# Loading the first rows in three pieces, splitting the first feed-forward slab by columns, and moving the rest columns behind the folded weights

## The chip, the cores and the metric

The kernel runs on one core of one Trainium2 chip. The metric is the device time of one execution in microseconds (us). It is some 1.3 us longer than the span that a profile shows, from the first instruction to the last. The first 512-column matmuls start 0.427 us apart and not 0.216 as later. "The clock turns" is said here for the change from the one step to the other.

## The reference

Two branches work on the same `x` (2048 tokens, 512 wide), and a gate mixes them. Cut to what matters:

```python
qkv = x @ wqkv                                   # 512 -> 3*512, 32 heads of 16
pq, pk = q @ w_phi, k @ w_phi                    # per head, 16x16
phi = concat(softmax(p), softmax(-p))            # for q and for k
kv, z = phi_k^T v, sum(phi_k)                    # over all tokens
a = (phi_q kv / (phi_q z + 1e-6)) @ wo           # linear attention
b = relu(x @ w1) @ w2                            # 512 -> 1376 -> 512
g = sigmoid(sum(x * gate_w))
out = g * a + (1 - g) * b
```

## The kernel before

The kernel is tuned. TensorE is kept busy from the first microsecond to the last; the other engines copy, exponentiate and normalise behind it. Two stages are touched by the change.

**The start.** The first 512 rows of `x` ("x0") are loaded plainly, in two halves, and transposed by TensorE (a matmul against the identity), because the transposing loads would come too late (the first one of `x` lands at 18.9 us). VectorE and ScalarE copy the transposed pieces from PSUM to `XT`. Then the first eight 128-column units of `x @ w1` are computed "slab by slab": slab `t` multiplies the `t`-th quarter of the inner dimension for all eight units, so that a slab needs only one row block of `w1`. All eight PSUM banks are in use, so a bank that held a transposed piece is free for its unit only after that piece has been copied.

```python
warm(5)                       # matmuls on constants, until data arrive
...
ea = xtr("a0", 0, (0, 1), 6, (("dve", 0, 1, "xa0"), ("dve", 1, 2, "xa1")))
c1 = ("a1", 0, (2, 3), 7, (("act", 0, 2, "xa2"),))
xtr(*c1, part=(0, 1))
eb = xtr("b0", 1, (0,), 2, (("act", 0, 1, "xb0"),))
ec = xtr(*c1, part=(2, 3))
ed = xtr("b1", 1, (1, 2), 1, (("act", 0, 2, "xb1"),))
...                           # the copies are emitted here
slab(0, range(4))             # 512 columns, units 0 to 3
for fn in xtr("b2", 1, (3,), 2, (("dve", 0, 1, "xb3"),)):   # bank 2: unit 6 waits for this copy
    fn()
slab(0, range(4, 8))
...
for t in range(1, NDT):
    slab(t)
```

**The folded weights.** `wq` and `wk` are multiplied by `w_phi` once ("pre", eight results, the even ones copied by VectorE and the odd ones by ScalarE). The first q/k tile (`atile(0)`) needs all eight copies. Value tiles (`vtile`) and the rest columns of `w1` with the gate column (`rest`) are put between as work that doesn't depend on them.

```python
hunit(0, 8)
hunit(0, 9, "dve")
vtile(0, "dve")
vtile(1, "act", nextbank())
for i in range(4):
    pre(i)
rest(0)
for i in range(4, 8):
    pre(i)
vtile(2, "dve")
...
for m in range(NT):
    atile(m)                  # first q/k tile for m == 0
    ...
```

The softmax here doesn't subtract the row's maximum and nothing guards it: scores larger than these inputs give would overflow.

## Time and profile before

| | before |
|---|---|
| median of the first three executions | 147.16 us |
| the execution that was profiled | 148.19 us (span 146.80) |
| TensorE busy | 143.2 us, 98% of the span |
| share of the chain of waits on TensorE | 95% |

The first lines of the profile's page for the kernel before (span, TensorE's busy time with its share and its count of instructions, and the chain of work that ended last, followed back from the last instruction, by engine; PE is TensorE, PEld its weight loads, DVE VectorE, ACT ScalarE, POOL GpSimd, SP the engine that issues the loads):

```profile
span 146.8 us, 2520 instructions
...
PE 143.2 (98%) x961; PEld 73.2 (50%) x978; DVE 92.3 (63%) x157; ACT 72.7 (49%) x125; POOL 52.0 (35%) x62
...
PE 95%; DMA 2%; DVE 1%; issue 1%; SPq 0%
```

TensorE bounds the kernel, so only its idle time and its slow time can be won. The timeline of the kernel before shows where those lie. Its columns are the start, the length of the merged stretch, engine, line, operation, output and input with their form, the count, and in brackets the idle time before with what ended it.

```profile
2.90 0.85 PE L239 MATMUL PS<-IDN,OT 128*128 128x128 bf16 x6
...
3.97 1.04 PE L239 MATMUL PS<-IDN,OT 128*128 128x128 bf16 x8 [0.22 <-DMA OT<-in_A_x_dram]
...
4.93 1.60 PE L528 MATMUL PS<-XT,W 128*128 128x512 bf16 x4
...
6.67 0.42 DVE L255 CAST XT<-PS 128x256 bf16<-128x256 f32 x1 [2.35 <-PE PS L239]
...
16.64 1.22 DVE L321 CAST WQK<-PS 128x480 bf16<-128x480 f32 x2 [0.38 <-PE PS L316]
...
17.07 0.86 PE L294 MATMUL PS<-W,XT 128*128 128x97 bf16 x16
17.72 0.88 PEld L316 LDWEIGHTS PS<-Wbd,PHQ 128*128 128x128 bf16 x16
17.77 1.00 PE L316 MATMUL PS<-Wbd,PHQ 128*128 128x120 bf16 x16
...
18.18 1.22 DVE L321 CAST WQK<-PS 128x480 bf16<-128x480 f32 x2 [0.31 <-PE PS L316]
...
18.82 0.81 PE L411 MATMUL PS<-WV,XT 128*128 128x512 bf16 x3
...
19.59 1.78 PE L336 MATMUL PS<-WQK,XT 128*128 128x480 bf16 x8
19.67 0.69 DVE L419 CAST VS<-PS 128x512 bf16<-128x512 f32 x1 [0.27 <-PE PS L411]
```

Three readings. The transposes (L239) wait for the second half of x0 at 3.97. The first four 512-column matmuls (L528, from 4.93) span 1.60 us, which is twice as slow as later. Two VectorE copies of folded weights run from 18.18 to 19.40, and the first q/k matmul (L336) starts right behind, at 19.59; VectorE copies value tile 2 (L419) only after them.

Starts of single instructions in the trace give the gaps exactly. Matmuls overlap in the trace (a 512-column one is shown 0.379 us long at the full clock), so gaps are read from start to start: two 512-column matmuls in a row start 0.216 us apart at the full clock and 0.427 us apart before it turns. TensorE has four gaps in the whole execution: 0.43 and 0.13 us before the first slab, 0.25 us at 6.9, 0.12 us at 19.5. (A single step of 0.43 us here and there later is taken for a missing record and not a gap: the page counts 978 weight loads but 961 matmuls.)

### The profile page before, as it was taken

To read this page: it belongs to the slowest core of one execution; us is meant where nothing else is said; L and a number is where in the kernel's file an instruction comes from. 1 tells how busy PE (TensorE), PEld (TensorE's weight loads), DVE (VectorE), ACT (ScalarE), POOL (GpSimd) and SP (SyncE) were. 2 spreads that over 40 slices of the span, in tenths; PEclk is the share of its full clock that TensorE was granted. 3 is DMA by queue.
4 is the path that set the end of the run, shared out by engine and by line. 5 is a ranking of instruction groups with operands and counts; after the bars stand their busy time and mean duration, and the time that the engine had idled before them with its cause. 6 is when DMAs were issued, how large, how long until landed. Compare 5 with 4: busy or idle time off the path is not lost.

```text
span 146.8 us, 2520 instructions
## 1 busy us (share of the span) xinstructions
PE 143.2 (98%) x961; PEld 73.2 (50%) x978; DVE 92.3 (63%) x157; ACT 72.7 (49%) x125; POOL 52.0 (35%) x62
## 2 busy tenths in 40 slices
PE   8999999999999999999999999999999999999994
PEld 3444744444545545555645555554444444444443
DVE  3327746777688778678698976675444555555342
ACT  3307547887778778877878863022222111111150
POOL 2040001788768678787868820300000000000000
DMA  6999991033449965335843531454343322322213
GB/s 197 295 258 214 180 263 23 0 71 71 76 86 304 178 198 92 71 71 107 43 107 71 107 71 21 90 107 110 74 94 82 75 71 67 80 71 74 71 44 106
DMA packets 45221, 16.12 MB, mean 110 GB/s; under 512 B 39352, under 2 KB 44568, under 8 KB 45208
## 3 DMA queue, kind: packets, MB, share of 16 engines
q1 hardware_dynamic: 45056, 15.92, 49.6%
q8 instruction: 8, 0.13, 0.4%
q10 hardware_dynamic: 152, 0.03, 0.1%
q14 instruction: 5, 0.04, 0.1%
HBM read 4.41 MB, written 2.10 MB: 44 GB/s over the span
## 4 chain that ended last, share of the span: by engine, by line
PE 95%; DMA 2%; DVE 1%; issue 1%; SPq 0%
PE PS L490 25%; PE PS L282 19%; PE PS L336 18%; PE PS L499 9%; PE PS L411 9%; PE PS L528 5%; PE PS L465 3%; PE PS L433 3%; DMA OT<-in_A_x_dram 2%; PE PS L294 2%; PE PS L316 1%; PE PS L239 1%; DVE WQK L513 1%; DVE XT L255 0%; SPq L162 0%
## 5 line engine op out<-in xcount | busy, mean ns | idle before, releaser
L490 PE MATMUL PS<-W,HT 128*128 128x512 bf16 (+4 forms) x181 | 40.0, 366 | 0.3
L379 POOL TENSOR_TENSOR EB<-EB,SC 128x1024 bf16<-128x1024 bf16 x15 | 28.9, 1927 | 25.0 <-DVE SC L377 25.0
L355 ACT ACTIVATE EB<-PS 128x480 bf16<-128x480 f32 (+1 forms) x44 | 30.1, 757 | 15.1 <-PE PS L336 15.1
L504 ACT ACTIVATE TFA<-PS,GT 128x512 bf16<-128x512 f32 x16 | 11.0, 687 | 42.7 <-PE PS L499 36.6
L282 PE MATMUL PS<-XT,W 128*128 128x512 bf16 x124 | 30.0, 379 | 0.2
L336 PE MATMUL PS<-WQK,XT 128*128 128x480 bf16 x128 | 28.5, 366 | 0.0
L375 DVE TENSOR_REDUCE ZB<-EB 128x64 f32<-128x1024 bf16 x15 | 18.3, 1220 | 14.0 <-ACT EB L355 14.0
L513 DVE SCALAR_TENSOR_TENSOR WQK<-PS,OMG,TFA 128x512 bf16<-128x512 f32 (+2 forms) x17 | 12.2, 719 | 23.6 <-ACT TFA L504 22.4
L490 PEld LDWEIGHTS PS<-W,HT 128*128 128x128 bf16 (+1 forms) x187 | 17.0, 98 | 17.4
L268 ACT ACTIVATE HT<-PS 128x512 bf16<-128x512 f32 x35 | 20.3, 616 | 7.6 <-PE PS L528 5.7
L336 PEld LDWEIGHTS PS<-WQK,XT 128*128 128x128 bf16 x128 | 12.5, 98 | 14.0 <-DVE WQK L321 0.4
L390 DVE TENSOR_REDUCE ZB<-EB 128x64 f32<-128x1024 bf16 x16 | 18.6, 1164 | 0.0
L282 PEld LDWEIGHTS PS<-XT,W 128*128 128x128 bf16 x128 | 12.0, 98 | 13.2
L399 POOL TENSOR_TENSOR EB<-EB,SC 128x512 bf16<-128x512 bf16 x16 | 16.9, 1056 | 1.3
L499 PE MATMUL PS<-WO,OT 128*128 128x512 bf16 x63 | 16.0, 378 | 0.1
L411 PE MATMUL PS<-WV,XT 128*128 128x512 bf16 x59 | 15.3, 378 | 0.3
L475 DVE TENSOR_TENSOR WQK<-PS,RDEN 128x512 bf16<-128x512 f32 x16 | 11.1, 691 | 0.5
L499 PEld LDWEIGHTS PS<-WO,OT 128*128 128x128 bf16 x64 | 6.1, 97 | 7.2
L421 ACT ACTIVATE VS<-PS 128x512 bf16<-128x512 f32 x14 | 8.5, 610 | 2.0 <-PE PS L411 2.0
L377 DVE RECIPROCAL SC<-ZB 128x64 f32<-128x64 f32 x16 | 8.9, 553 | 0.5
L528 PE MATMUL PS<-XT,W 128*128 128x512 bf16 x31 | 7.9, 400 | 0.1
L411 PEld LDWEIGHTS PS<-WV,XT 128*128 128x128 bf16 x64 | 5.5, 97 | 4.9
(57 smaller groups left out, 87.2 us busy)
## 6 DMA issues: line engine op xcount, KB each, us to landing
out_dram<-WQK SPq DMA_DIRECT2D x15, 128.0 KB, 1.7
W<-in_B_w_dram SPq DMA_DIRECT2D x3, 256.0 KB, 4.5
W<-in_B_w_dram SPq DMA_DIRECT2D x2, 384.0 KB, 5.3
OT<-in_A_x_dram SPq DMA_DIRECT2D x2, 256.0 KB, 3.0
WV<-in_A_wqkv_dram SPq DMA_DIRECT2D x1, 512.0 KB, 6.3
W<-in_B_w_dram SPq DMA_DIRECT2D x1, 512.0 KB, 4.5
WO<-in_A_wo_dram SPq DMA_DIRECT2D x2, 256.0 KB, 3.0
W<-in_B_w_dram SPq DMA_DIRECT2D x1, 352.0 KB, 5.8
```

Of the source, the lines that this page charges most:

```text
L268: p.op("act", lambda e: e.activation(dst, src, ACT.Relu), after=[f"h{c}_{kt}"], ev=ev)
L282: p.op("pe", lambda e, t=t: e.matmul(PS[:, bank, :], W1[:, t, kt * P:(kt + 1) * P], XT[:, t, c * 512:(c + 1) * 512], start=(t == 0), stop= ...
L336: p.op("pe", lambda e, dt=dt, which=which: e.matmul(PS[:, which, 0:DE], XT[:, dt, m * P:(m + 1) * P], WQK[:, which, dt * DE:(dt + 1) * DE] ...
L355: p.op("act", lambda e: e.activation(dst, s_, ACT.Exp, scale=scale), after=[f"qk{m}"] + busy, ev=ev)
L375: p.op("dve", lambda e: e.tensor_reduce(zk, ek, AX.X, ALU.add), after=[emk, f"cst{b}"], ev=f"zk{m}")
L379: p.op("pool" if m < NT - 1 else "dve", lambda e: e.tensor_tensor(EB[:, b, 3, :].rearrange("p (g f) -> p g f", f=DH), EB[:, b, 2, :].rearr ...
L390: p.op("dve", lambda e: e.tensor_reduce(ZB[:, b, 0:64].rearrange("p (h s) -> p h s", s=2), bass.AP(tensor=EB, offset=base, ap=[[EBS, P], [ ...
L399: p.op("pool", lambda e: e.tensor_tensor(EB[:, b, 0, :].rearrange("p (h s f) -> p h s f", h=H, s=2)[:, :, 1, :], EB[:, b, 1, :].rearrange( ...
L411: p.op("pe", lambda e, dt=dt: e.matmul(PS[:, bank, :], XT[:, dt, m * P:(m + 1) * P], WV[:, dt, :], start=(dt == 0), stop=(dt == NDT - 1)), ...
L490: p.op("pe", lambda e, kt=kt, M=M: e.matmul(PS[:, bank, 0:n], HT[0:M, kt, m * P:(m + 1) * P], W2[0:M, kt, cs], start=(kt == 0), stop=(kt = ...
L499: p.op("pe", lambda e, t=t: e.matmul(PS[:, bank, :], OT[:, t, m * P:(m + 1) * P], WO[:, t, :], start=(t == 0), stop=(t == NDT - 1)), after ...
L528: p.op("pe", lambda e, u=u: e.matmul(PS[:, UB[u], :], W1[:, t, u * P:(u + 1) * P], XT[:, t, 0:512], start=(t == 0), stop=(t == NDT - 1)), ...
```

## The change

The intent, as the diff shows it: work on three quarters of the rows while the last quarter is still loading, and hide the latency of the folded-weight copies behind more work. A third, small part loads `W2` in two pieces in place of three. The diff, cut:

```diff
+        XJ = ((0, 2), (2, 3), (3, 4))
         def loadx0(h):
-            ... XS[:, 2 * h:2 * h + 2, :] ...
+            j0, j1 = XJ[h]
+            ... XS[:, j0:j1, :] ...
         loadw1(0, 0, 4 * P, "a")
+        loadx0(2)
         loadw1(0, 4 * P, 8 * P)
 ...
         def slab(t, us=range(8), c0=0, c1=512):      # now on columns c0 to c1
 ...
+        for dt in range(1, 4):
+            xtr(1, dt, 6, (dt - 1) * P)
+        xev("act", 1, 1, 3, 6)
+        slab(0, range(4), 0, 384)
+        for dt in range(4):
+            xtr(2, dt, 1, dt * P)                    # last quarter, into bank 1
+        xev("dve", 2, 0, 4, 1)                       # one 128x512 copy on VectorE
+        slab(0, range(4, 8), 0, 384)                 # unit 7 uses bank 1
+        slab(0, range(8), 384, 512)
 ...
         for i in range(4):
             pre(i)
-        rest(0)
+        vtile(2, "dve")
         for i in range(4, 8):
             pre(i)
-        vtile(2, "dve")
+        rest(0)
 ...
-                for a, b in ((0, 4), (4, 7), (7, KU)):
+                for a, b in ((0, 5), (5, KU)):
```

More of the change, by code (lines that the diff above doesn't have):

```diff
@@ L159, in orow @@
             return oq[:, m, :] if m < 4 else o2[m * P:(m + 1) * P, :]
+        XJ = ((0, 2), (2, 3), (3, 4))
         def loadx0(h):
-            p.dma("sp", lambda e: e.dma_start(out=XS[:, 2 * h:2 * h + 2, :], in_=xq[:, 2 * h:2 * h + 2, :]),
-                  f"x0{h}", ev=f"x0{h}")
+            j0, j1 = XJ[h]
+            p.dma("sp", lambda e: e.dma_start(out=XS[:, j0:j1, :], in_=xq[:, j0:j1, :]), f"x0{h}", ev=f"x0{h}")
         def loadw1(t, c0=0, c1=DFF, tag=""):
@@ L220, in xready @@
         def xready(c):
-            return ["xa0", "xa1", "xa2", "xb0", "xb1", "xb3"] if c == 0 else [f"x{c}"]
+            return ["xv00", "xv01", "xv02", "xv10", "xv11", "xv20"] if c == 0 else [f"x{c}"]
         def gatecol(bank):
@@ L233, in warm @@
                      after=["one"])
-        def xtr(nm, h, dts, bank, evacs, part=None):
-            n = 2 * len(dts)
-            for i in (range(n) if part is None else part):
-                dt, j = dts[i // 2], 2 * h + i % 2
-                p.op("pe", lambda e, i=i, dt=dt, j=j: e.matmul(
-                    PS[:, bank, i * P:(i + 1) * P], XS[:, j, dt * P:(dt + 1) * P], IDN[:, :],
-                    start=True, stop=True),
-                    after=["idn", f"x0{h}"] + (free[bank] if i == 0 else []), ev=(f"xt{nm}" if i == n - 1 else None))
-            if part is not None and n - 1 not in part:
-                return []
-            return xev(nm, h, dts, bank, n, evacs)
@@ L247, in xev, with xtr @@
-        def xev(nm, h, dts, bank, n, evacs):
-            src = PS[:, bank, 0:n * P].rearrange("p (t c) -> p t c", c=256)
-            out = []
-            for eng, i0, i1, ev in evacs:
-                d = XT[:, dts[i0]:dts[i0] + i1 - i0, h * 256:(h + 1) * 256]
-                s = src[:, i0:i1, :]
-                if eng == "dve":
-                    out.append(lambda d=d, s=s, ev=ev: p.op(
-                        "dve", lambda e: e.tensor_copy(d, s), after=[f"xt{nm}"], ev=ev))
-                else:
-                    out.append(lambda d=d, s=s, ev=ev: p.op(
-                        "act", lambda e: e.activation(d, s, ACT.Copy), after=[f"xt{nm}"], ev=ev))
-            free[bank] = [evacs[-1][3]]
-            return out
+        def xtr(h, dt, bank, off):
+            for j in range(*XJ[h]):
+                o = off + (j - XJ[h][0]) * P
+                p.op("pe", lambda e, j=j, o=o: e.matmul(
+                    PS[:, bank, o:o + P], XS[:, j, dt * P:(dt + 1) * P], IDN[:, :], start=True, stop=True),
+                    after=["idn", f"x0{h}"] + (free[bank] if off == 0 else []),
+                    ev=(f"xt{h}{dt}" if j == XJ[h][1] - 1 else None))
@@ new lines, in xev @@
+        def xev(eng, h, dt, n, bank):
+            j0, j1 = XJ[h]
+            w = (j1 - j0) * P
+            d = XT[:, dt:dt + n, j0 * P:j1 * P]
+            s = PS[:, bank, 0:n * w].rearrange("p (t c) -> p t c", c=w)
+            ev = f"xv{h}{dt}"
+            if eng == "dve":
+                p.op("dve", lambda e: e.tensor_copy(d, s), after=[f"xt{h}{dt + n - 1}"], ev=ev)
+            else:
+                p.op("act", lambda e: e.activation(d, s, ACT.Copy), after=[f"xt{h}{dt + n - 1}"], ev=ev)
+            free[bank] = [ev]
@@ L522, in bass_gated_mix__linear_kernel_hedgehog__dense_activation_relu__prompt_kernel, with slab @@
         UB = (3, 4, 5, 0, 6, 7, 2, 1)
-        XA = ("xa0", "xa1", "xa2", "xa2")
-        XB = ("xb0", "xb1", "xb1", "xb3")
-        def slab(t, us=range(8)):
+        XV = (("xv00", "xv01", "xv02", "xv02"), ("xv10", "xv11", "xv11", "xv11"), ("xv20",) * 4)
+        def slab(t, us=range(8), c0=0, c1=512):
+            hs = [h for h in range(3) if XJ[h][0] * P < c1 and XJ[h][1] * P > c0]
             for u in us:
                 p.op("pe", lambda e, u=u: e.matmul(
-                    PS[:, UB[u], :], W1[:, t, u * P:(u + 1) * P], XT[:, t, 0:512],
-                    start=(t == 0), stop=(t == NDT - 1)),
-                    after=["w10a" if t == 0 and u < 4 else f"w1{t}", XA[t], XB[t]] + free[UB[u]],
+                    PS[:, UB[u], c0:c1], W1[:, t, u * P:(u + 1) * P], XT[:, t, c0:c1],
+                    start=(t == 0 and c0 == 0), stop=(t == NDT - 1), skip_group_check=True),
+                    after=["w10a" if t == 0 and u < 4 else f"w1{t}"] + (free[UB[u]] if c0 == 0 else [])
+                    + [XV[h][t] for h in hs],
                     ev=(f"h0_{u}" if t == NDT - 1 else None))
@@ L537, in bass_gated_mix__linear_kernel_hedgehog__dense_activation_relu__prompt_kernel @@
         warm(1, 384)
-        ea = xtr("a0", 0, (0, 1), 6, (("dve", 0, 1, "xa0"), ("dve", 1, 2, "xa1")))
-        c1 = ("a1", 0, (2, 3), 7, (("act", 0, 2, "xa2"),))
-        xtr(*c1, part=(0, 1))
-        eb = xtr("b0", 1, (0,), 2, (("act", 0, 1, "xb0"),))
-        ec = xtr(*c1, part=(2, 3))
-        ed = xtr("b1", 1, (1, 2), 1, (("act", 0, 2, "xb1"),))
-        for fn in (ea[0], eb[0], ea[1], ec[0], ed[0]):
-            fn()
-        slab(0, range(4))
-        for fn in xtr("b2", 1, (3,), 2, (("dve", 0, 1, "xb3"),)):
-            fn()
-        slab(0, range(4, 8))
+        xtr(0, 0, 6, 0)
+        xtr(0, 1, 7, 0)
+        xtr(0, 2, 2, 0)
+        xtr(1, 0, 1, 0)
+        xtr(0, 3, 2, 256)
+        xev("dve", 0, 0, 1, 6)
+        xev("dve", 0, 1, 1, 7)
+        xev("act", 1, 0, 1, 1)
+        xev("act", 0, 2, 2, 2)
+        for dt in range(1, 4):
[7 more added lines that the diff above has]
+        slab(0, range(8), 384, 512)
         for b in range(VB):
```

## The prediction

> **What bounds it now.** TensorE: the page gives PE 143.2 of 146.8 us (98%), and the chain of waits is 95% PE. Instruction starts in the trace show only four true PE gaps, all before 20 us: 0.43 us at 3.54 (second half of x0 lands at 3.92), 0.13 at 4.80 (slab waits for a ScalarE copy of transposed x ending 4.78), 0.25 at 6.9 (the unit in bank 2 waits for the VectorE copy ending 7.10), and 0.12 at 19.47 (first q/k tile waits for folded-weight copies ending 19.40 on VectorE, 19.45 on ScalarE). After 20 us 512-column matmuls follow each other every 0.216 us without a hole. So about 0.9 us is all there is to win; a 2% change (2.9 us) is not available.
>
> Before 6.1 us 512-column matmuls start 0.427 us apart, afterwards 0.216. The Trainium skill ("TensorE: Matmul & The Clock Gate", Part 1) describes this gate: half rate until a busy window of about 3.4 us has passed, windows free-running. The trace agrees on the two rates. I assume that the switch stays near 6.1 us.
>
> **Start.** Landings were 2.72 (256 KB), 3.92 (512 KB in all), 4.26 (640), 5.31 (768), so the second x0 load (384 KB in all) should land near 3.3. The 0.43 us gap goes. Transposes run to 4.18; the 128-column ScalarE copy ends near 4.2, so the slab starts near 4.3, not 4.93. But four 384-column matmuls at the cold rate (0.32 each) end at 5.6, four transposes at 6.0, and their single 128x512 VectorE copy (0.69 us; the smaller one removed took 0.425) near 6.95. Bank 1 serves that copy and unit 7, so unit 7 waits until about 7.0: a new gap of about 0.45 us, at the warm rate. Then 0.16 plus eight 128-column matmuls at about 0.056 (120-column ones with own weights ran at 0.053): slab 1 starts near 7.6; before, 7.59. The early gain, made at the cold rate, is given back at the new wait: net about 0 (-0.15 to +0.2).
>
> **Folded weights.** Before: pre 0-3 (0.84 us), rest columns (0.69), pre 4-7 (0.84), value tile 2 (0.86), q/k tile. After, the value tile stands in the middle and the rest columns at the end. VectorE's order becomes copies 0, 2, value-tile copy (0.69 us), copies 4, 6 (0.61 each). Counted from the first pre matmul: value tile done at 1.86, its copy 1.90-2.59, copy 4 to 3.20, copy 6 to 3.81, q/k tile near 3.9. PE work ends at 3.23, so the gap grows from 0.12 to about 0.65 us. Before, the q/k tile started at 3.36. Loss about 0.55 us, straight onto the span, because PE has no later hole to absorb it.
>
> One more load issue (0.43 us of SP) delays the transposing loads by that; they landed at 13.2, 15.3, 18.9 and were first used at 16.2, 17.8, 22.1: no wait. W2 in two pieces instead of three: nothing.
>
> **Prediction: 147.6 us, 80% range 146.9 to 148.1.** Faster by over 2%: 0.01; within: 0.98; slower by over 2%: 0.01.
>
> **Right if** the timeline shows the slab starting near 4.3, a PE gap near 6.6-7.0 ended by the VectorE copy of x, slab 1 near 7.6, and a gap of about 0.6 us before the first q/k tile, ended by the VectorE copy of folded weights.
>
> **Wrong if** the PE clock turns full well before 6.1 us, now that PE idles less: then the x copy comes earlier and the start gains up to 0.8 us; if the second load lands after 3.6; or if the folded-weight copies aren't held up by the value-tile copy, so that the move gains its 0.12 us, about 147.0 in all.

## The result, and the profile after

| | before | after |
|---|---|---|
| median of six executions each | 147.31 us | 148.15 us |
| lowest and highest | 147.10, 147.55 | 147.72, 148.38 |
| ratio | 1 | 1.0052, 95% interval 1.003 to 1.0074 |
| span of the profile | 146.80 us | 146.80 us |

A ratio here is the mean time of one kernel's fast runs over that of the other's in the same rounds, so it is not quite the ratio of the medians. The changed kernel is 0.5% slower. That is within 2%, and clear of zero. The ratio times the 147.16 us known at the time gives 147.93 us, inside the predicted range; the raw median of 148.15 lies 0.05 us beyond its upper end, on rounds in which the kernel before ran 0.15 us higher too.

Yet the two profiles have *the same* span. One of them must be untypical, and it is the one of before: at 148.19 us its execution is above all six timed ones.

The page of the changed kernel:

```profile
span 146.8 us, 2536 instructions
...
PE 142.6 (97%) x969; PEld 73.6 (50%) x986; DVE 92.5 (63%) x157; ACT 72.6 (49%) x125; POOL 52.2 (36%) x62
...
PE 93%; DMA 2%; DVE 2%; issue 1%
```

The chain of waits of the changed kernel, at the start (columns: start, length, what the end waited for):

```profile
1.09 3.59 DMA W<-in_B_w_dram
4.68 0.05 issue
4.73 0.82 PE PS L524 x4
5.55 0.24 PE PS L241 x4
5.79 0.02 issue
5.81 0.69 DVE XT L253
...
6.56 2.94 PE PS L524 x19
```

The first slab (L524) starts at 4.73, behind the first piece of `w1`, for which TensorE waited 0.46 us. Its four matmuls take 0.82 us together and not 1.28: the clock is already full. Then everything waits for the single 128x512 copy of the last quarter (L253), as the prediction had it; TensorE stands still from 6.10 to 6.56. Slab 1, the second, starts at 7.18.

The timeline of the changed kernel in the fold stage (from the first folded-weight matmul to the first q/k matmul):

```profile
16.23 1.22 DVE L317 CAST WQK<-PS 128x480 bf16<-128x480 f32 x2 [0.38 <-PE PS L312]
...
17.52 1.00 PE L312 MATMUL PS<-Wbd,PHQ 128*128 128x120 bf16 x16
17.72 0.69 DVE L415 CAST VS<-PS 128x512 bf16<-128x512 f32 x1 [0.27 <-PE PS L407]
...
18.33 1.21 DVE L317 CAST WQK<-PS 128x480 bf16<-128x480 f32 x2
18.36 0.86 PE L290 MATMUL PS<-W,XT 128*128 128x97 bf16 x16
...
19.59 1.33 PEld L332 LDWEIGHTS PS<-WQK,XT 128*128 128x128 bf16 x8 [0.53 <-DVE WQK L317]
19.59 1.79 PE L332 MATMUL PS<-WQK,XT 128*128 128x480 bf16 x8 [0.38 <-DVE WQK L317]
```

The value tile's copy (L415) now stands in front of the last two folded-weight copies on VectorE. These run from 18.33 to 19.54. The rest columns (L290) end their issue at 19.05, and the first q/k matmul waits until 19.59: a gap of 0.54 us where before there was one of 0.12.

Two markers are enough to account for a profile: where the second slab starts, and how long it is from the first folded-weight matmul to the first q/k matmul. Once both are taken off the span, the same remainder is left in all six profiles of this start and fold, within 0.04 us (the other four are experiments told below):

| profile | clock full from about | second slab starts | fold stage | span | remainder |
|---|---|---|---|---|---|
| before | 6.1 | 7.60 | 3.36 | 146.80 | 135.84 |
| before, a second profile | 3.2 | 6.70 | 3.36 | 145.89 | 135.84 |
| after | 4.1 to 4.7 | 7.18 | 3.78 | 146.80 | 135.83 |
| start alone | 5.7 | 7.45 | 3.36 | 146.64 | 135.82 |
| fold alone | 4.0 | 6.79 | 3.78 | 146.43 | 135.86 |
| after, one copy later | 4.1 to 4.3 | 6.85 | 3.50 | 146.18 | 135.83 |

So nothing is given back or lost after 20 us, and the third part of the change (`W2` in two pieces) is not visible. The equal spans of before and after are 0.42 us gained on the second slab, where the clock turned 1.4 us or more earlier, and 0.42 us lost in the fold stage.

### The profile page after: what moved, and what is told of

The parts are those of the page before. It is cut to its first block, busy times and chain, and to the rows that moved or that the text cites. A ratio compares the mean times of both kernels' runs of the same rounds, so it can differ in the third digit from the quotient of the medians.

```text
span 146.8 us, 2536 instructions
## 1 busy us (share of the span) xinstructions
PE 142.6 (97%) x969; PEld 73.6 (50%) x986; DVE 92.5 (63%) x157; ACT 72.6 (49%) x125; POOL 52.2 (36%) x62
## 4 chain that ended last, share of the span: by engine, by line
PE 93%; DMA 2%; DVE 2%; issue 1%
PE PS L486 25%; PE PS L278 19%; PE PS L332 18%; PE PS L495 9%; PE PS L407 9%; PE PS L524 5%; PE PS L461 3%; PE PS L429 3%; DMA W<-in_B_w_dram 2%; PE PS L290 1%; DVE WQK L509 1%; PE PS L312 1%; DVE XT L253 0%; DVE VS L415 0%; DVE WQK L317 0%
## 5 line engine op out<-in xcount | busy, mean ns | idle before, releaser
L486 PE MATMUL PS<-W,HT 128*128 128x512 bf16 (+3 forms) x182 | 40.2, 366 | 0.3
L278 PE MATMUL PS<-XT,W 128*128 128x512 bf16 x124 | 30.2, 379 | 0.2
L524 PE MATMUL PS<-XT,W 128*128 128x512 bf16 (+2 forms) x39 | 7.4, 336 | 0.6 <-DVE VS L554 0.3
```

What stands on the lines that cost most here:

```text
L278: p.op("pe", lambda e, t=t: e.matmul(PS[:, bank, :], W1[:, t, kt * P:(kt + 1) * P], XT[:, t, c * 512:(c + 1) * 512], start=(t == 0), stop= ...
L486: p.op("pe", lambda e, kt=kt, M=M: e.matmul(PS[:, bank, 0:n], HT[0:M, kt, m * P:(m + 1) * P], W2[0:M, kt, cs], start=(kt == 0), stop=(kt = ...
L524: p.op("pe", lambda e, u=u: e.matmul(PS[:, UB[u], c0:c1], W1[:, t, u * P:(u + 1) * P], XT[:, t, c0:c1], start=(t == 0 and c0 == 0), stop=( ...
```

## The experiments

Twelve kernels ran, in three sets of four; all gave correct results. The sets ran on different chips, so ratios are compared inside a set first.

### 1. The kernel before, again

No edit.

> The kernel before, unchanged, against itself: what the spread of one and the same program is, and when its TensorE clock turns full. In the profiled execution of before the 512-column matmuls went from 0.427 to 0.216 us spacing at 6.1 us and that execution took 148.19 us, while the timed ones took 147.1 to 147.55; in the profile of the changed kernel the full rate was there by 4.7 us. Theory A (the switch belongs to the execution, not to the kernel): this profile may show the switch at another place, and the time moves by half the shift (up to about 1 us). Rival B (the changed start makes the clock turn earlier): the switch is at 6.1 us again. Ratio 1.000 within 0.003 in both.

Measured: 147.25 us median of six (147.20 to 147.96), ratio 0.999 (0.9959 to 1.0021). The same program's executions thus lie up to 0.8 us apart here, and the eleven executions of before in this set lie between 147.09 and 148.19. The chain of waits of this profile:

```profile
4.60 1.02 PE PS L528 x4
...
5.77 0.42 DVE XT L255
...
6.25 5.79 PE PS L528 x26
```

The four first matmuls that took 1.60 us in the first profile take 1.02 us here. Starts in the trace show the full rate from 3.2 us on, against 6.1 us. The span is 0.90 us shorter, and the second slab starts 0.90 us earlier. So the turn of the clock belongs to the execution and not to the kernel: theory A. It also means that the profile on which the prediction was based showed the late end of what one program does by itself.

### 2. The changed start alone

The fold order and the `W2` pieces are as before, the rest as after:

```diff
-        vtile(2, "dve")
+        rest(0)
         for i in range(4, 8):
             pre(i)
-        rest(0)
+        vtile(2, "dve")
```

> The changed start alone; fold order and the W2 pieces as before. My theory: the early gain is eaten by the wait for the last x copy. With the switch of the clock at the same moment as before, the second slab starts 0.0 to 0.2 us later than in before, so ratio 1.000 to 1.002 (0 to +0.3 us). Rival: the start is the whole loss (+0.8 us, ratio 1.005). Other rival: it gains 0.4 us (second slab at 7.18 in the profile after, 7.59 before), ratio 0.997.

Measured: 147.87 us median (147.58 to 148.17), ratio 1.0026 (0.9992 to 1.0059). The point estimate is +0.38 us, but the interval runs from -0.1 to +0.9 us: inconclusive, though a gain of 0.4 us is outside it. The chain of waits of its profile:

```profile
4.42 1.38 PE PS L524 x4
...
6.08 0.69 DVE XT L253
```

The clock turned at 5.7, the slab started at 4.34, the wait for the last x copy was 0.46 us, and the second slab started at 7.45, which is 0.15 us ahead of the first profile of before, with a clock that turned 0.4 us earlier. Before the turn 512-column matmuls take twice the time (0.427 against 0.216 us), so by estimate a turn 0.4 us earlier is worth about 0.2 us; at the same clock the two starts are then level within 0.05 us, as the prediction summed it for a turn near 6 us.

### 3. The changed fold order alone

The kernel before with the three lines of the fold order exchanged, and nothing else.

> The changed order of value tile 2 and the rest columns alone. My theory: a PE gap of 0.53 us before the first q/k tile in place of 0.12 us, ended by the VectorE copies of the folded weights; first pre matmul to first q/k matmul 3.78 us in place of 3.36, so +0.4 us, ratio 1.0028. Rival: the order is neutral (ratio 1.000) and the start makes the loss.

Measured: 147.78 us median (147.71 to 148.44), ratio 1.0031 (0.9998 to 1.0063), so +0.45 us by the point estimate. The profile: gap 0.54 us, fold stage 3.78 us, exactly as in the changed kernel, and it is the VectorE copies that end it, as its chain of waits shows:

```profile
17.33 0.67 DVE VS L419
...
18.50 0.66 DVE WQK L321
...
19.20 1.79 PE PS L336 x8
```

The +0.42 us of the fold stage are shown by the profile; the interval of the timing just includes zero.

### 4. The changed kernel with the value tile's copy put later

TensorE's order is that of the changed kernel; only VectorE's order changes.

```diff
-        vtile(2, "dve")
+        vtile(2, "dve", copy=False)      # matmuls here ...
         for i in range(4, 8):
             pre(i)
+        vtile(2, "dve", mm=False)        # ... the copy here
         rest(0)
```

> The changed kernel with one thing moved: VectorE copies value tile 2 after the last folded-weight copy, not between; TensorE's order stays. My theory (the value tile's copy on VectorE holds the folded copies up by up to 0.69 us): the gap before the first q/k tile falls from 0.53 us to 0.1 to 0.3 us, first pre to first q/k matmul 3.4 to 3.55 us, and the time is 0.3 us better than the changed kernel's, ratio to before about 1.003. Rival (the rest columns, 0.69 us, simply cover less of the copies' latency than the value tile's 0.86 us, whatever VectorE's order): the gap stays above 0.4 us.

Measured: 147.44 us median (147.31 to 148.17), ratio 1.0006 (0.9974 to 1.0038). The timeline of this kernel:

```profile
17.60 1.22 DVE L317 CAST WQK<-PS 128x480 bf16<-128x480 f32 x2 [0.48 <-PE PS L312]
...
18.74 0.68 DVE L417 CAST VS<-PS 128x512 bf16<-128x512 f32 x1
...
18.96 1.34 PEld L332 LDWEIGHTS PS<-WQK,XT 128*128 128x128 bf16 x8 [0.22 <-DVE WQK L317]
```

The last two folded-weight copies start as soon as their matmuls are done, the gap falls to 0.26 us and the fold stage to 3.50 us. Of the 0.42 us, 0.28 were VectorE's order. The other 0.14 remain, and fit the rest columns (0.69 us of TensorE work) standing where the value tile (0.86 us) stood; that part was not tested by itself. The time came out better than the expected ratio of 1.003: +0.09 us, interval -0.4 to +0.6. This kernel has the changed start too, so with 0.14 us taken off for the fold stage its time leaves -0.5 to +0.4 us for the start.

### 5 to 8. A first attempt to hold the clock still

To compare starts without the clock's moment, four kernels got 25 more warm-up matmuls, and the first loads waited for the twentieth of them:

```diff
-        warm(5)
+        warm(20, ev="pin")
+        warm(10)
 ...           # the loads of x0 and of the gate column: after=["pin"]
```

The fourth also carried an attempt at a better version of the change: 384 columns of three units of the second slab fill the wait for the last x copy, and value tile 1 takes the place in the middle of the fold stage, so that value tile 2 can follow the rest columns:

```diff
-        slab(0, range(4, 8), 0, 384)
+        slab(0, range(4, 7), 0, 384)
+        slab(1, range(3), 0, 384)
+        slab(0, (7,), 0, 384)
         slab(0, range(8), 384, 512)
+        slab(1, range(3), 384, 512)
+        slab(1, range(3, 8))
 ...
-        vtile(1, "act", nextbank())
         for i in range(4):
             pre(i)
-        vtile(2, "dve")
+        vtile(1, "act", nextbank())
         for i in range(4, 8):
             pre(i)
         rest(0)
+        vtile(2, "dve")
```

> The kernel before with 25 more warm-up matmuls, on whose twentieth the first loads wait: the same start, but moved some 6 us later and with TensorE's clock full in every execution. Theory A (the spread of 147.1 to 148.2 us comes from the moment at which the clock turns): the executions of this one agree within 0.2 us; ratio to before about 1.04 to 1.06, of no interest in itself; it is the base for the other three. Rival: the spread stays near 1 us, so it comes from the loads or from elsewhere.

> The changed start alone, with the same pinned warm clock. My theory: with the clock full the first slab is short, the wait for the last x copy (0.46 us) and the wait for the first w1 piece stay, so slab 1 starts 0.15 to 0.5 us later than in before_warm and the time is 0.15 to 0.5 us longer. Rival (the start is neutral whatever the clock, as the prediction summed it): within 0.1 us of before_warm.

> The whole change with the same pinned warm clock. My theory: 0.42 us longer than start_warm (the fold stage, 3.78 in place of 3.36 us), so 0.55 to 0.9 us longer than before_warm. Rival (the W2 pieces or later stages matter too): differs from start_warm by less than 0.3 or more than 0.55 us.

> The changed kernel with both new waits filled, with the pinned warm clock: while VectorE copies the last x piece, TensorE does 384 columns of three units of the second slab; in the fold stage value tile 1 takes the middle place and value tile 2 goes back to the end, behind the rest columns. My theory: no PE gap near the last x copy, none before the first q/k tile; 0.4 to 0.5 us better than start_warm in the start, 0.5 better than after_warm in the fold stage: 0.1 to 0.4 us shorter than before_warm. Rival (the wait only moves on, to the second w1 load or to the ScalarE copies): not shorter than before_warm.

Measured, medians of six: 154.52 (154.02 to 154.91), 154.58 (153.53 to 155.26), 154.84 (154.51 to 155.10) and 155.33 us (154.62 to 156.22). The spread was *not* smaller, and that was a fault of the design: twenty matmuls take longer when the clock turns late (the first load was issued at 7.82, 7.58, 6.88 and 7.06 us in the four profiles), so the hold moved with the very thing that it was to remove. The times decide nothing. The profiles are of use, taken from the first load issue: the second slab starts 6.51 us after it in the first, 6.83 in the second and 6.71 in the third. So the start of the change is 0.32 and 0.20 us worse here. In the second profile TensorE waited 0.53 us for the second piece of `w1`, which the change issues behind the third piece of x0 and which landed at 13.26. The fold stage of the third shows its 0.54 us gap again.

The fourth is a failure with a clear cause. The chain of waits of its profile:

```profile
18.37 6.90 DMA PHQ<-in_A_wqkv_dram
...
25.31 1.01 PE PS L312 x16
```

TensorE waited 1.69 us in the middle of the fold stage for the second transposing load of `wqk`, which came late in this profile (25.26), and another 0.7 us for the second row block of `w1` (landed 13.48, the filling work started at 13.52). The rival was right: work that is moved forward needs its own data forward too. What it does show is that with the value tile last, the first q/k matmul follows without a gap.

### 9 to 12. The clock held properly, and two fillings

Now the first load waits for a chain of eight VectorE memsets, whose length does not depend on TensorE's clock, and TensorE does 39 warm-up matmuls meanwhile. The fillings, in the kernel *before*: the last two units of the first slab swap banks, so that the wait for the last x copy falls on the last unit, and value tile 3 is computed ahead of the first q/k tile.

```diff
+        for i in range(8):
+            p.op("dve", lambda e, i=i: e.memset(HT[:, i, :], 0.0), ev="pin" if i == 7 else None)
 ...
-        warm(5)
+        warm(39)
 ...           # the fillings:
-        UB = (3, 4, 5, 0, 6, 7, 2, 1)
+        UB = (3, 4, 5, 0, 6, 7, 1, 2)
 ...
         vtile(2, "dve")
+        vtile(3, "act", nextbank())
 ...
-            if m + 3 < NT:
+            if 0 < m < NT - 3:
                 vtile(m + 3)
```

> The kernel before, with the first load held back by a chain of eight VectorE memsets of fixed length (about 9 us) while TensorE does 39 warm-up matmuls instead of 5, so that the clock has turned before the loads start and the start of the loads does not depend on when it turned (in the four runs before this it did, since they waited on matmuls). Theory A (the spread of before is the moment of the turn): executions agree within 0.3 us. Rival: the spread stays near 1 us. From the first x0 issue to the first full-width matmul of the second slab: 6.5 to 6.75 us, as in the other warm profiles of this start (6.61, 6.71, 6.51).

Measured: five executions were recorded, 156.00 to 156.24 us. The spread of 0.24 us, against 0.95 us for the eleven unheld executions of before in the same set (147.15 to 148.10), agrees with theory A: in the kernel before, most of the spread goes with the moment at which the clock turns. From the first load issue to the second slab: 6.48 us.

> The changed start alone, held back in the same way. Profiles of the changed start with a warm clock gave 7.10, 6.77, 6.34 and 6.66 us from the first x0 issue to the second slab, against 6.5 to 6.7 with the start of before. Theory 1 (neutral, as the prediction summed it): time within 0.15 us of before_pinned. Theory 2 (the start loses about half of what the whole change lost, because the early gain shrinks at the full clock and the wait for the last x copy does not): 0.2 to 0.5 us longer than before_pinned.

(Two of the figures in this expectation were misread: for 6.34 and 6.66 the traces give 6.83 and 6.71.)

Measured: 156.93 us median of six, but from 155.88 to 157.65. The medians differ by 0.80 us. Two of the six, 157.31 and 157.65, are among the three executions with a mean granted clock of 0.989; the median of the other four is 156.45, 0.3 us above before_pinned, but they still lie 1.4 us apart. The profiled execution (156.29, against 156.00 for the profile of before_pinned) has the second slab 6.73 us after the first load issue, 0.25 us later than in before_pinned, and a span 0.28 us longer. The chains of the two profiles, first the start of before:

```profile
10.04 3.32 DMA W<-in_B_w_dram
13.35 0.05 issue
13.40 1.04 PE PS L530 x4
...
14.58 0.42 DVE XT L257
...
15.07 5.79 PE PS L530 x26
```

and the changed start:

```profile
10.05 3.23 DMA W<-in_B_w_dram
13.27 0.05 issue
13.32 0.82 PE PS L526 x4
...
14.40 0.69 DVE XT L255
...
15.15 5.96 PE PS L526 x33
```

Both slabs start behind the first piece of `w1`, which was issued at the same place in the queue's program and lands at the same time: the changed start gains 0.08 us there, and the longer copy on VectorE takes more than that back, so that the wait ends 0.09 us later (15.15 against 15.07). The larger part comes after it. The change leaves unit 7's 384 columns and the last 128 columns of all eight units behind the wait, 0.62 us from its end to the second slab, where before it was two units, 0.44 us. So more work stands behind the rows that arrive last. But the fastest execution of all belongs to the changed start, and the slower ones were not profiled. In this profile the second `wqk` load landed at 25.94 us (24.34 in before_pinned), just when its matmuls were due; that it came later still in the slow executions is likely but not shown.

> The kernel before, held back in the same way, with two of its own gaps filled: the last two units of the first slab swap banks, so that the one which waits for the last x copy is the last one (0.2 of the 0.25 us gap), and value tile 3 is computed ahead of the first q/k tile in place of after it (the 0.12 us gap). If TensorE gaps pass to the span one for one, 0.30 us (0.2 to 0.35) shorter than before_pinned. Rival (they are taken back later, by loads or copies): within 0.1 us of it.

Measured: 157.11 us median (156.64 to 158.59), a loss of 1.0 us against before_pinned where a gain of 0.3 was expected. The slowest execution is the third with a clock of 0.989.

> The same two fillings in the kernel before as it is, without the hold: expected 0.3 us (0.2%) shorter than before, ratio 0.998, which the spread of 1 us may hide; fastest executions at 146.8 us in place of 147.1. Rival: ratio 1.000 and fastest executions at 147.1.

Measured: 148.28 us median (147.94 to 148.64), ratio 1.0037 (1.0016 to 1.0059): slower. The 0.25 us gap in the slab fell to 0.03, and the 0.12 us gap before the first q/k tile is gone. The chain of waits of this profile shows two new ones:

```profile
21.36 1.84 ACT EB L355 x2
...
23.25 0.78 PE PS L336 x3
...
88.34 0.60 ACT HT L268
...
89.08 2.10 PE PS L490 x9
```

The value tile that was moved forward had been the work under which ScalarE's two exponentials of the first tile (1.84 us) ran; the second q/k tile now waits 0.36 us for them. And, by the code, the extra step of the bank rotation left the first output matmuls (L490) on a bank that ScalarE had yet to empty: 0.69 us. Together these waits cost more than the two gaps were worth. So no kernel of this study beats the kernel before. The bank swap was not run by itself.

## Why the prediction was right or wrong

**What bounds the kernel, and how much can be won: right.** TensorE; nothing happened after 20 us, as the constant remainder of the table shows.

**The wait for the last x copy: right.** Predicted about 0.45 us, ended by a 0.69 us VectorE copy; measured 0.46 us in the changed kernel and in the start alone, 0.35 us in the kernel with the later copy.

**The slab starts near 4.3: right in two of three profiles.** It started at 4.34 twice and at 4.73 in the profile after, where the first piece of `w1` landed at 4.68 (the second load of x0 landed at 3.16, near the predicted 3.3). The Trainium skill ("DMA: Bandwidth & Descriptors", "Why a DMA increments its semaphore by 16 and not by 1") says that a load counts as landed only when all its engines have finished. The trace agrees: the first of the sixteen finished that piece at 3.07, the last at 4.68.

**"I assume that the switch stays near 6.1 us": the step that failed.** The clock turned between 3.2 and 6.3 us in the fourteen profiles, and by a matter of the execution. The Trainium skill ("TensorE: Matmul & The Clock Gate", Part 1) calls the windows free-running. The prediction quoted it and did not draw the consequence, that one profile shows one draw. The range seen here, 3.1 us, fits windows of about 3.4 us. With a turn near 6 us the start of the change is level within 0.05 us, by the estimate of experiment 2. With a full clock, the second slab starts 6.48 to 6.71 us after the first load issue in the four profiles with the start of before, and 6.71 to 7.10 us in the five with the changed start (means 6.58 and 6.83 us). So there the term "net about 0" was too kind by some 0.25 us, by the profiles. The prediction had also said that an early turn would make the start gain up to 0.8 us; the start of before gains from it as well, 0.90 us between its two profiles.

**Fold stage: right in its mechanism, a little too large.** Predicted a gap of 0.65 and a loss of 0.55 us; measured 0.54 and 0.42. The mis-sized term is the row of VectorE copies, added up as 0.69 + 0.61 + 0.61 us. They start 0.61 and 0.57 us apart though they last 0.69 and 0.65, since a copy that waits for nothing starts before the one ahead of it has ended. The Trainium skill ("Perfetto Trace Analysis", "Optimizing Scalar/DVE Operations") says that the write-acknowledgement part of an instruction's profiled latency overlaps with the next instruction, and the trace agrees, with an overlap of 0.08 us. From the start of the first to the end of the last the three took 1.82 us and not 1.91, which is 0.09 of the 0.12 us by which the q/k tile came before its predicted moment (3.78 us after the first folded-weight matmul and not 3.9).

**The total.** Predicted +0.44 us, measured +0.77 (0.0052 of 147.3 us). The fold stage is 0.42 of it, shown by the profiles of three kernels. What is left is 0.35 us, for the start. The start alone agrees (+0.38, interval -0.1 to +0.9), and so do the profiles with a full clock (+0.25); a late turn (+0.05) and the time of experiment 4 (-0.5 to +0.4) speak for less. How it divides between the start, the scatter of the loads' landings and the luck of the clock stays open: it would take a profile of many executions. That the predicted total fitted is in part luck: the fold stage was put 0.13 us too high and the start some 0.3 us too low, and these errors worked against each other.

## What to carry to other kernels

Ask first whether the profiled execution is a typical one: if its time is away from the median of the others, find out what differs before costing anything in it. Work put between a producer and its consumer must be looked at on every engine it uses: the value tile hid latency on TensorE and made it on VectorE. And a gap that is filled by moving work forward has to be paid where that work stood, and needs its data and its bank earlier.

## What the Trainium skill lacked or had wrong

- "TensorE: Matmul & The Clock Gate", Part 1, gives the two rates and the free-running windows rightly (0.427 and 0.216 us per 512 columns here). It puts the turn at about 4 us of sustained activity, 500 ns either way; here it came 2.8 to 5.9 us after the first matmul. That is nearer to another sentence of the same part, by which one kernel had 6, 11 or 14 slow matmuls. Its advice that the ramp is under 1% of a typical span, and that no particular count should be fitted, holds (0.9 of 146 us between two profiles of one program), but this is more than the whole change was worth, and it makes the time of a single execution useless for effects of half a per cent.
- "DMA: Bandwidth & Descriptors" gives no time for which SP is held by issuing one plain load. Here it is 0.34 to 0.43 us for each load of x0 and `w1`, for 128 KB as for 256 KB, and 0.51 us for the 16 KB of `w_phi`. With the one load more of the change, `w_phi` was issued 0.48 us later (4.32 against 3.84) and the first transposing load 0.34 us later (5.42 against 5.08).
- The same page says that the sixteen engines of one load finish independently, but not how far apart. For the 128 KB piece of `w1` it was 0.8 us in one profile (3.45 to 4.26, before) and 1.6 us in another (3.07 to 4.68, after).
